# An attention-and-FFN kernel: k, q and v loaded first, x formed earlier in the order, float32 w_out for two more items

## The chip, the cores and the metric

The program runs on one core of a Trainium2 chip. Its engines are PE (TensorE, the matmuls, with a queue of its own for loading weights, PEld), DVE (VectorE), ACT (ScalarE), POOL (GpSimd) and SP (SyncE, which here only issues DMAs). Each takes its own instructions strictly in the order in which they were queued when the kernel was built, and waits where an instruction's data aren't there yet. The metric is the device time of one execution in microseconds.

## The reference

Attention with a softmax of q over the head's features and a softmax of k over the sequence, and on its result a feed-forward layer:

```
q_s = exp(q - max(q, axis=-1));  q_s = q_s / (sum(q_s, axis=-1) + 1e-09)
k_s = exp(k - max(k, axis=2));   k_s = k_s / (sum(k_s, axis=2) + 1e-09)
kv  = einsum('bhsd,bhse->bhde', k_s, v)
x   = einsum('bhsd,bhde->bhse', q_s, kv)        # then (B*S, H*D)
h   = x @ w_in
g   = h * erf(max(h, 0) + log1p(exp(-abs(h))))  # erf of softplus
out = g @ w_out
```

There are 8 batches, 8 heads, 576 rows and 64 features, so x is 4608 x 512; w_in is 512 x 2048 and w_out 2048 x 512. Inputs q, k and v are float32. The weights arrive as float64 and are read as pairs of int32.

## The kernel before

**Work items.** The 4608 rows of x are cut into 12 blocks of 384 tokens (three for each pair of batches), and the 2048 hidden columns into 4 groups g of 512. A block and a group make a work item n; there are 48, four in a row for each block. An item has these steps: `m n.0` to `m n.3` (mm1, the product with w_in, into tile H), T and G (softplus and erf on ACT, into tile G), U (gmul on DVE: G times H), I and O (ghi and glo on DVE, which split G into two float16 tiles that lie in H's place), and `M n.0` to `M n.2` (mm2, the product with w_out, for three tiles of 128 tokens, summed over the block's four items in the PSUM banks o0 to o2).

**Two arithmetics.** Items 0 to 3 (the first block) are computed wholly in float32, with the decoded weights as they are (mm1_32 L912, mm2 L988). All others use weights and x split into a high and a low float16 part. mm1 is then seven products of half-size blocks (L873, twelve 128x192 matmuls each, into banks pX, pY and pZ, evacuated at L885 to L900 by DVE and ACT in turn), and mm2 has 36 matmuls an item (L997).

**The weights.** Each of the eight weight groups (jobs 0 to 7: in 0, in 1, out 0, in 2, out 1, in 3, out 2, out 3) is loaded as two pieces of 1 MB (wload, L182) and decoded from float64 bits to float32 by three DVE operations a piece (L198, L202, L205; step `D job.piece`). ACT squares them for their maxima (Q, L230), and when all eight are squared, Z (wscales) computes the scales: a reduction (L240), transposes (L245), further reductions (L249) and a row of tiny operations (L252 to L273). Then each group is split (S: high part on ACT at L278, low part on DVE at L279) and, for w_in, the sums of blocks that the seven products need are formed (R, L304). Items 4 on can't start before Z, S0 and R0.

**Attention.** The opening (function start) treats batch 0: per half of the heads q is reduced and normalised (L758, L442 to L448), the maximum of k over the sequence is taken (k_max, L477 and L480), turned by PE and reduced (kT L487, km L491, kB L500), subtracted (L745, L747), exponentiated (L754), and k is multiplied with v (kv, L521), normalised (kvbd, L550) and multiplied with the transposed q (qT L596, x L605) into x (L424). Batches 1 to 7 go through a generator whose pieces are called off by `A` in the order list, and later by a pace.

**What sets the order.** The string ORDER lists the steps up to item 3, SPLITS the splits behind items 4 to 6, and a loop the rest. A scheduler moves instructions within each engine's queue from there. SP's DMAs share eight semaphores, so that each waits for the eighth before it. H has three buffers, G two, and the pool `at` gives two to each tag.

Of the kernel before, what the change touches and what calls it, by code (L numbers as in the profile page):

```python
# [53 lines left out]
def attn_moe_kernel(  # L54
# [54 lines left out]
    WT = [  # L109
        cp.tile([P, 2 * (7 if which == "in" else 4) * 512], F16, name=f"wt{i}")  # L110
        for i, (which, g) in enumerate(JOBS)
    ]
# [39 lines left out]
    slots += [None, 0, 1, *range(4, 2 * NG), -1]  # L152

    def wload():

# [2 lines left out]
        while i < NPC * NJ and slots:
            w = slots.pop(0)
            if i >= NPC * (NJ - 1 if w is None else NJ if w < 2 else w - 2):  # L160
                continue
            if w == -1:
                w, other = None, "x7"
            else:
                other = None
            which, g = wjobs[i // NPC]
            a = i % NPC
            if which == "in":
                src = w_in[a * 2 * P:(a + 1) * 2 * P, 2 * g * 512:2 * (g + 1) * 512]
            else:  # L170
                src = w_out[(4 * g + 2 * a) * P:(4 * g + 2 * a + 2) * P, :]
            if other:

                raws[i] = xp.tile([P, 2, 1024], I32, tag=other, name=f"raw_{i}")
            elif w is None:
                raws[i] = rp.tile([P, 2, 1024], I32, tag="raw", bufs=1, name=f"raw_{i}")
            else:
                raws[i] = WT[w][:, :4096].bitcast(I32).rearrange("p (a n) -> p a n", a=2)
            held[i] = -1 if other else w

            eng = nc.sync if i < LOADS.count("w") else nc.gpsimd
            eng.dma_start(raws[i], src.rearrange("(a p) n -> p a n", p=P))  # L182
            nxt[0] += 1
            return
# [964 lines left out]
```

## Time and profile before

| What | Value |
|---|---|
| Times of three runs | 886.32, 883.01, 882.18 us (median 883.01) |
| Profiled execution: its own time, and the span in the trace | 886.16 us, 884.3 us |
| Mean granted TensorE clock | 0.983 |
| PE, DVE, ACT, POOL busy | 828.4, 656.3, 504.6, 17.7 us |
| DMA traffic | 55.52 MB, mean 63 GB/s |
| First f32 matmul of item 0 | 34.40 us |
| First mm2 of item 0 | 58.75 us |
| First f16 matmul of item 4 | 137.80 us |

Times in the trace are counted from the span's start. A busy PE says that a matmul was under way, not that it ran at full rate: the granted clock stands beside it. [...]

### The profile page before, as it was taken

How to read it: one execution, taken by the hardware profiler on the slowest of the kernel's cores; microseconds unless marked ns; L12 is line 12 of the kernel's file. 1: busy time of each engine (PE TensorE's matmuls, PEld its weight loads, DVE VectorE, ACT ScalarE, POOL GpSimd, SP SyncE). 2: the span in 40 equal slices, each digit the busy share in tenths (PEclk: the TensorE clock that was granted, in tenths of full speed). 3: DMA queues.
4: the chain of work that ended last, by engine and by line, in shares of the span. 5: the costliest groups of instructions: out<-in, count | busy, mean ns of one | idle time of the engine just before them, and what ended most of it. 6: DMA issues, size and time to landing. Idle time of an engine off the chain costs nothing.

```text
span 884.3 us, 15529 instructions
## 1 busy us (share of the span) xinstructions
PE 828.4 (94%) x6556; PEld 571.0 (65%) x6556; DVE 656.3 (74%) x901; ACT 504.6 (57%) x645; POOL 17.7 (2%) x37
## 2 busy tenths in 40 slices
PE   2899995799989989999999999999999999999997
PEld 1555553666657757767767667767776677676763
DVE  7899669998978696876886596877885565744453
ACT  2487376786565645644754646645745546453632
POOL 2100100000000000000000000000000000000000
PEclk9899997799999999999999999999999999999999
DMA  9984720013105120421023111311010000000100
GB/s 274 408 186 137 178 47 37 1 40 81 43 24 114 37 60 10 94 61 25 14 72 79 36 49 25 90 48 25 13 49 1 13 24 2 27 11 1 36 1 36
DMA packets 117381, 55.52 MB, mean 63 GB/s; under 512 B 106561, under 2 KB 108609, under 8 KB 117313
## 3 DMA queue, kind: packets, MB, share of 16 engines
q1 hardware_dynamic: 115136, 46.15, 20.2%
q0 software_dynamic: 2176, 8.39, 2.6%
q8 instruction: 51, 0.84, 0.4%
q14 instruction: 18, 0.14, 0.1%
HBM read 45.09 MB, written 9.44 MB: 62 GB/s over the span
## 4 chain that ended last, share of the span: by engine, by line
PE 67%; DVE 19%; ACT 9%; issue 2%; DMA 2%; SPq 1%; ACTq 0%; DVEq 0%
PE o L997 27%; PE pX L873 15%; PE pZ L873 7%; PE o L988 4%; ACT G L326 4%; PE pY L873 3%; ACT L326 3%; DVE G L952 3%; DVE H L969 2%; PE kv L521 2%; DVE kmax L477 2%; PE pX L912 2%; DVE wt L279 2%; PE qT L596 1%; DVE H L965 1%
## 5 line engine op out<-in xcount | busy, mean ns | idle before, releaser
L997 PE MATMUL o<-wt,H 128*128 128x512 f16 x1584 | 367.7, 381 | 3.2 <-DVE H L965 2.3
L873 PEld LDWEIGHTS <-wt 128*128 128x128 f16 x3696 | 312.8, 99 | 50.3 <-issue 18.8
L997 PEld LDWEIGHTS <-H 128*128 128x128 f16 x1584 | 152.8, 98 | 159.6 <-DVE H L965 3.3
L873 PE MATMUL pX<-x,wt 128*128 128x192 f16 x2112 | 207.5, 249 | 9.4 <-DVE H L887 3.6
L326 ACT ACT_TABLE_LOAD x104 | 133.4, 1283 | 11.9 <-DVE H L898 7.2
L952 DVE SCALAR_TENSOR_TENSOR G<-G,small,H 128x1536 f32<-128x1536 f32 x44 | 79.9, 1816 | 67.0 <-ACT G L326 66.9
L873 PE MATMUL pZ<-x,wt 128*128 128x192 f16 x1056 | 105.6, 250 | 8.7 <-ACT H L890 4.5
L900 ACT COPY H<-pX 128x384 f32<-128x384 f32 x44 | 21.0, 476 | 131.4 <-PE pX L873 131.4
L326 ACT ACTIVATE G<-H,U 128x768 f32<-128x768 f32 (+1 forms) x60 | 73.0, 1232 | 25.7 <-DVE H L898 25.1
L969 DVE TENSOR_TENSOR H<-G,H 128x1536 f16<-128x1536 f32 x44 | 77.2, 1756 | 1.1
L326 ACT ACTIVATE G<-G 128x1536 f32<-128x1536 f32 x48 | 71.3, 1484 | 0.5
L873 PE MATMUL pY<-x,wt 128*128 128x192 f16 x528 | 51.6, 246 | 3.5 <-ACT wt L278 2.0
L424 ACT ACTIVATE x<-x 128x384 f32<-128x384 f32 (+1 forms) x52 | 17.6, 386 | 55.4 <-PE x L608 53.3
L885 DVE COPY H<-pY 128x384 f32<-128x384 f32 x44 | 24.3, 553 | 28.8 <-PE pY L873 28.8
L278 ACT ACTIVATE x<-x 128x768 f16<-128x768 f32 (+1 forms) x44 | 32.9, 762 | 21.5 <-DVE x L370 21.4
L965 DVE CAST H<-G 128x1536 f16<-128x1536 f32 x44 | 42.0, 955 | 0.8
L279 DVE SCALAR_TENSOR_TENSOR x<-x,x 128x768 f16<-128x768 f32 (+1 forms) x44 | 37.2, 848 | 3.5 <-ACT x L278 3.4
L1013 DVE TENSOR_SCALAR ob<-o,V 128x512 f32<-128x512 f32 x29 | 21.7, 747 | 23.7 <-PE o L997 23.6
L898 DVE TENSOR_TENSOR H<-pZ,H 128x384 f32<-128x384 f32 x44 | 24.2, 551 | 19.6 <-PE pZ L873 19.5
L887 DVE TENSOR_TENSOR H<-pX,H 128x384 f32<-128x384 f32 x44 | 24.4, 554 | 14.8 <-PE pX L873 14.4
L370 DVE TENSOR_TENSOR x<-x 128x384 f32<-128x384 f32 x44 | 24.2, 550 | 8.5 <-ACT x L424 8.1
L895 DVE TENSOR_TENSOR H<-pX,H 128x384 f32<-128x384 f32 x44 | 24.2, 550 | 4.5 <-PE pX L873 4.4
(160 smaller groups left out, 824.5 us busy)
## 6 DMA issues: line engine op xcount, KB each, us to landing
out_dram<-ob SPq DMA_DIRECT2D x32, 256.0 KB, 2.2
vbuf<-in_v_dram SPq DMA_DIRECT2D x60, 128.0 KB, 3.2
q<-in_q_dram SPq DMA_DIRECT2D x56, 128.0 KB, 3.0
k<-in_k_dram SPq DMA_DIRECT2D x56, 128.0 KB, 3.2
wt<-in_moe_w_out_dram POOLq DMA_DIRECT2D x5, 1024.0 KB, 6.7
wt<-in_moe_w_in_dram SPq DMA_DIRECT2D x4, 1024.0 KB, 8.7
raw<-in_moe_w_in_dram SPq DMA_DIRECT2D x2, 1024.0 KB, 16.4
wt<-in_moe_w_out_dram SPq DMA_DIRECT2D x2, 1024.0 KB, 13.5
```

Of the source, the lines that this page charges most:

```text
L278: nc.scalar.activation(hi, src, AF.Copy, scale=s)
L279: nc.vector.scalar_tensor_tensor(lo, src, s, hi, op0=ALU.mult, op1=ALU.subtract)
L326: i = nc.scalar.activation(out_, in_, func, **kw)
L370: nc.vector.tensor_tensor(Bk[o], Bk[a], Bk[b], op=ALU.subtract)
L873: nc.tensor.matmul(o, w[wl][:, c, a * P:(a + 1) * P], x[:, xl, xi, c, :], start=(new and a == 0 and c == 0 and i == 0), stop=(c == 1 and i ...
L885: nc.vector.tensor_copy(C[0, 0], bank2("Y"))
L887: add(C[0, 0], bank2("X"), C[0, 0], op=ALU.add)
L952: nc.vector.scalar_tensor_tensor(flat(s["G"]), flat(s["G"]), GA[:, g:g + 1], flat(s["H"]), op0=ALU.mult, op1=ALU.mult,)
L965: nc.vector.tensor_copy(flat(s["gh"]), flat(s["G"]))
L969: nc.vector.tensor_tensor(flat(s["gl"]), flat(s["G"]), flat(s["gh"]), op=ALU.subtract)
L988: nc.tensor.matmul(o, s["G"][:, a, ts_], w[:, a, :], start=(first_ and a == 0), stop=(last_ and a == FG - 1),)
L997: nc.tensor.matmul(o, s[gt][:, a, ts_], w[wl][:, a, :], start=(first_ and a == 0 and i == 0), stop=(last_ and a == FG - 1 and i == 2),)
```

## The change

Line numbers of the kernel after differ from those before; where a row of it is shown, its operation is named.

1. **Loads.** k, q and v are loaded ahead of all weights, and the first eight weight pieces behind them on SP. The ninth and tenth go through POOL's queue, the ninth at once behind the opening's memsets. Weight places are new tiles (four wi, five wo) and the free places are sorted by the time up to which they are free.
2. **k_max** takes two tensor-tensor maxima per half (128x512 and 128x256) instead of one strided reduction.
3. **The first weight piece of each half is decoded in two column halves**, and `m0.0` and `m0.1` need the first half only.
4. **x of batch 0** is formed from kvbd directly after the second normalisation. Its columns for block 0 are evacuated at once (x0 to x3), those for block 1 after the scale is known (y0 to y3). q of batch 0 is transposed into banks pX, pY, pZ and o2.
5. **Scales.** The squares go to a bfloat16 tile in SBUF, the transposes of Z to pY and pZ; a factor GB, for unsplit w_out, is added to the tiny operations. The scheduler places Z earlier (below).
6. **Items 4 and 5** (OUT32) multiply G with GB and w_out of groups 0 and 1 in float32, without ghi and glo. S2 and S4, the splits of these two groups, move behind items 7 and 8.

```diff
-LOADS = "qkwwvwwwwww"
+LOADS = "kqvwwwwwwww"
...
-    qm0 qm1 kmax kT kB qe0 qn0 ks2 ks0 D0.0 ks1 ke2 ke0 ke1 w6 kv0 kn0 D0.1 qe1 qn1 kv1 t0
-    kn1 kvs x0 t1 lkv t2 x2 t3 x1 x3
-    m0.0 D1.0 m0.1 D1.1 m0.2 m0.3 T0 G0 Q0
+    kmax qm0 kT kB qe0 qm1 ks2 ks0 ks1 ke2 ke0 ke1 qn0 t0 t1 qe1 qn1 w6 kv0 kn0 kv1 kn1
+    D0.0.0 D0.1.0 t2 t3 x0 x1 x2 x3 kvs lkv y0 y1 y2 y3
+    m0.0 m0.1 D0.0.1 D0.1.1 D1.0 D1.1 m0.2 m0.3 T0 G0 Q0
...
-    M2.0 M2.1 M2.2 M3.0 M3.1 M3.2 S1 R1 S2
+    M2.0 M2.1 M2.2 M3.0 M3.1 M3.2 S1 R1
...
-SPLITS = {4: "S3 R3 S4", 5: "S5 R5 S6", 6: "S7"}
+SPLITS = {4: "S3 R3", 5: "S5 R5 S6", 6: "S7", 7: "S2", 8: "S4"}
+
+OUT32 = range(4, 6)
+OUTS = [2, 3, 0, 1]
...
+        if part is None:
+            r = raws[i].rearrange("p a n -> p (a n)").rearrange("p (n two) -> p n two", two=2)
+        else:
+            r = raws[i][:, :, 512 * part:512 * part + 512].rearrange(
+                "p a (n two) -> p a n two", two=2
+            )
+            d = d.rearrange("p (a n) -> p a n", a=2)[:, :, 256 * part:256 * part + 256]
...
-                bank(f"sq_{jn}_{i}"), stg[jn][:, i * 512:(i + 1) * 512], AF.Square,
-                accum_out=sq4[:, o, i:i + 1],
+                sqs, stg[jn][:, i * 512:(i + 1) * 512], AF.Square, accum_out=sq4[:, o, i:i + 1]
...
-            bk = psa.tile([P, 512], F32, tag="bk", name=f"ws_{which}")
+            bk = psh.tile([P, 512], F32, tag="pY" if i == 0 else "pZ", name=f"ws_{which}")
...
+        nc.vector.tensor_scalar(
+            GB, w_u["in"], m[:, 0:1], m[:, 1:2], op0=ALU.mult, op1=ALU.mult
+        )
+        nc.vector.tensor_scalar_mul(GB, GB, 2.0**-20)
...
         kmax = at.tile([P, H, D], F32, tag="qT", name=f"kmax_{b}")
+        k2 = at.tile([P, 2, 4, D], F32, tag="qT", name=f"k2_{b}")
         for hf in range(2):
-            nc.vector.tensor_reduce(
-                kmax[:, hf * 4:hf * 4 + 4, :], ks[hf], axis=AX.X, op=ALU.max
+            nc.vector.tensor_tensor(k2, ks[hf][:, 0:2], ks[hf][:, 2:4], op=ALU.max)
+            nc.vector.tensor_tensor(
+                kmax[:, hf * 4:hf * 4 + 4, :], k2[:, 0], k2[:, 1], op=ALU.max
             )
...
         def xc(c):
-            bk = pso.tile([P, 512], F32, tag=f"o{(c + 1) % 2}", name=f"x_0_{c}")
+            name = f"x_0_{c}"
+            bk = pso.tile([P, 512], F32, tag=f"o{c}", name=name) if c < 3 else bank(name)
             x_mm(0, c, bk, r[f"t{c}"])
-            x_split(0, c, bk)
+            x_split(0, c, bk, slice(1))
+            put(f"x{c}", bk)
...
-            steps[f"x{i}"] = (f"t{i} kvs", lambda i=i: xc(i))
+            steps[f"x{i}"] = (f"t{i} kn1", lambda i=i: xc(i))
+
+            steps[f"y{i}"] = (f"x{i} kvs", lambda i=i: x_split(0, i, r[f"x{i}"], slice(1, 9)))
...
+        assert "all" in wready
         nc.vector.scalar_tensor_tensor(
-            flat(s["G"]), flat(s["G"]), GA[:, g:g + 1], flat(s["H"]),
+            flat(s["G"]), flat(s["G"]), (GB if n in OUT32 else GA)[:, g:g + 1], flat(s["H"]),
             op0=ALU.mult, op1=ALU.mult,
         )
-        assert "all" in wready
+        if n in OUT32:
+            return
...
-        if n < NG:
+        if n < NG or n in OUT32:
             w = stg[jn].rearrange("p (a e) -> p a e", a=FG)
...
-            if 4 < n <= N and i < 2:
+            if 4 < n <= N and i < 2 and n - 1 not in OUT32:
                 tok(f"{'IO'[i]}{n - 1}")
```

**First place: DVE's queue at the start of the program.** A row has the line, the operation, what it writes and reads (buffer 101 holds the first raw half of q before, and the first of k after; 103, 105 and 107 hold the other halves; km is the reduced turned maximum), and the shape. Before:

```order
L758 TENSOR_REDUCE q_0_0_m_141<-H_raw_0_0_101 128x16
L759 TENSOR_TENSOR q_0_0_137<-H_raw_0_0_101,q_0_0_m_141 128x1024
L758 TENSOR_REDUCE q_0_1_m_144<-G_raw_0_1_103 128x16
L477 TENSOR_REDUCE kmax_0_147<-H_raw_0_0_105 128x256
L477 TENSOR_REDUCE kmax_0_147<-H_raw_0_1_107 128x256
L442 TENSOR_REDUCE q_0_0_r_164<-q_0_0_137 128x16
L480 TENSOR_TENSOR kmax_0_147<-kmax_0_147,kt_0_109 64x512
```

and after:

```order
L496 TENSOR_TENSOR k2_0_140<-H_raw_0_0_101 128x512
L497 TENSOR_TENSOR kmax_0_139<-k2_0_140 128x256
L496 TENSOR_TENSOR k2_0_140<-H_raw_0_1_103 128x512
L497 TENSOR_TENSOR kmax_0_139<-k2_0_140 128x256
L500 TENSOR_TENSOR kmax_0_139<-kmax_0_139,kt_0_105 64x512
L511 TENSOR_REDUCE km_0_154<-kT_0_149 128x4
L782 TENSOR_REDUCE q_0_0_m_146<-H_raw_0_q_100 128x16
```

The chain of k now stands first, and q's reductions behind it; the two reductions of k have become two pairs of maxima.

**Second place: DVE's queue where the scales are computed**, beside items 2 and 3 (small holds the scales, sq4 the squares, ws are the turned maxima, wse their steps, x_1 and x7_1 the x of block 1, and q_2_0 and q_2_1 the halves of q of batch 2; the last number of a name is the buffer). Before:

```order
L435 TENSOR_REDUCE q_2_1_m_1225<-q_2_1_782 128x16
L436 TENSOR_TENSOR q_2_1_782<-q_2_1_782,q_2_1_m_1225 128x1024
L240 TENSOR_REDUCE small_84<-sq4_100 128x8
L279 SCALAR_TENSOR_TENSOR x7_1_861<-x_1_140,x7_1_861 128x384
L249 TENSOR_REDUCE wse_in_822<-ws_in_817 128x4
L249 TENSOR_REDUCE wse_out_834<-ws_out_829 128x4
L252 TENSOR_SCALAR wse_in_822<-wse_in_822 128x4
```

and after:

```order
L988 TENSOR_TENSOR G_3_698<-G_3_698,H_3_664 128x1536
L297 SCALAR_TENSOR_TENSOR x7_1_837<-x_1_138,x7_1_837 128x768
L252 TENSOR_REDUCE small_81<-sq4_98 128x8
L387 TENSOR_TENSOR x_1_138<-x_1_138 128x2x192
L262 TENSOR_REDUCE wse_in_796<-ws_in_791 128x4
L262 TENSOR_REDUCE wse_out_808<-ws_out_803 128x4
L265 TENSOR_SCALAR wse_in_796<-wse_in_796 128x4
L453 TENSOR_REDUCE q_2_0_m_1092<-q_2_0_741 128x16
L266 TENSOR_SCALAR wse_in_796<-wse_in_796 128x4
```

The reduction of the squares (L240, now L252) stood behind both halves of batch 2's q; now it stands ahead of them, just behind the product of item 3 (L988), and the reduction of the first half (L453) stands between the scales' small operations.

**Third place: ACT's queue at item 9** (its copies of pZ and pX into H_9, table load and softplus; x_3 is the x of block 3, and x7_3 its split for item 12). Before:

```order
L890 COPY H_9_1784<-pZ_9_1837 128x2x192
L278 ACTIVATE x7_3_1978<-x_3_1639 128x768
L892 COPY H_9_1784<-pX_9_1799 128x2x192
L278 ACTIVATE x7_3_1978<-x_3_1639 128x384
L278 ACTIVATE x7_3_1978<-x_3_1639 128x768 x2
L900 COPY H_9_1784<-pX_9_1799 128x2x192
```

and after:

```order
L928 COPY H_9_1711<-pZ_9_1764 128x2x192
L296 ACTIVATE x7_3_1908<-x_3_1564 128x768
L930 COPY H_9_1711<-pX_9_1726 128x2x192
L296 ACTIVATE x7_3_1908<-x_3_1564 128x384
L938 COPY H_9_1711<-pX_9_1726 128x2x192
L343 ACT_TABLE_LOAD
L343 ACTIVATE G_9_1874<-H_9_1711,U_1_645 128x1536
L296 ACTIVATE x7_3_1908<-x_3_1564 128x768
```

The item's last copy (L900, now L938) stood behind two further splits of x (L278); they have moved behind it.

More of the change, by code (lines that the diff above doesn't have):

```diff
@@ L105, in attn_moe_kernel @@
         kvbd.append(t)
[L109 to L112, printed above, removed]
+    WI = [cp.tile([P, 2 * 7 * 512], F16, name=f"wi{g}") for g in range(NG)]
+    WO = [cp.tile([P, 2 * 4 * 512], F16, name=f"wo{g}") for g in range(NG + 1)]
+    wplace = {("out", g): WO[([NG] + OUTS)[OUTS.index(g)]] for g in range(NG)}
+    wplace |= {("in", g): WI[g] for g in range(NG)}
+    raw_place = {("out", g): WO[g] for g in range(NG)}
+    raw_place |= {("in", g): WI[g + 1] for g in range(NG - 1)}
     WIN = 7 * 512
@@ L154, in wload @@
+    slots.sort(key=lambda x: x[1])
     def wload():
         i = nxt[0]
[L158 to L163, printed above, removed]
-            else:
[L165 to L184, printed above, removed]
@@ L186, in wdecode @@
-    def wdecode(i):
-        jn, a = divmod(i, NPC)
-        if a == 0:
-            if jn + 2 < NJ:
-                stg[jn] = WT[jn + 2][:, :4096].bitcast(F32)
-            elif jn == NJ - 2:
+        if i == NPC * NJ:
+            return
+        while slots and i >= slots[0][1]:
+            slots.pop(0)
+        if not slots:
+            return
+        place, end = slots.pop(0)
+        which, g = wjobs[i // NPC]
+        a = i % NPC
+        if which == "in":
+            src = w_in[a * 2 * P:(a + 1) * 2 * P, 2 * g * 512:2 * (g + 1) * 512]
+        else:
+            src = w_out[(4 * g + 2 * a) * P:(4 * g + 2 * a + 2) * P, :]
@@ new lines, in wload, with wdecode @@
+        if place == "x7":
+            place = xp.tile([P, 4096], F16, tag="x7", name=f"raw_{i}")
+        raws[i] = place[:, :4096].bitcast(I32).rearrange("p (a n) -> p a n", a=2)
+        held[i] = [place, end]
+        eng = nc.sync if i < LOADS.count("w") else nc.gpsimd
+        eng.dma_start(raws[i], src.rearrange("(a p) n -> p a n", p=P))
+        nxt[0] += 1
+    def wdecode(i, part=None):
+        jn, a = divmod(i, NPC)
+        if jn not in stg:
+            if wjobs[jn] in raw_place:
+                stg[jn] = raw_place[wjobs[jn]][:, :4096].bitcast(F32)
+            else:
@@ L287, in wsplit @@
         s = w_s[which][:, g:g + 1]
-        assert "all" in wready and not raws and jn == nsplit[0]
-        nsplit[0] += 1
+        assert "all" in wready and not raws
+        assert all(wplace[wjobs[jn]] is not raw_place.get(wjobs[j]) for j in stg)
         if which == "out":
@@ L610, in x_mm, with x_split @@
             )
-    def x_split(b, c, bk):
-        for blk, off, o, w in xcols(b, 0 if b % 2 == 0 else SM + 2 * TAIL, SM):
+    def x_split(b, c, bk, part=None):
+        for blk, off, o, w in xcols(b, 0 if b % 2 == 0 else SM + 2 * TAIL, SM)[part or slice(9)]:
             x_put(
@@ L623, in attention @@
         ks, qs, kt = d["k"], d["q"], even["kt"][tl]
-        kmax = k_max(b, [t.rearrange("p t h d -> p h d t") for t in ks], (kt, tl))
+        kmax = k_max(b, ks, (kt, tl))
         yield SHARES[0]
@@ L782, in start @@
         steps = {
-            "kmax": ("", lambda: put("kmax", k_max(
-                0, [t.rearrange("p h t d -> p h d t") for t in kx], (kt, tl)))),
+            "kmax": ("", lambda: put("kmax", k_max(0, perm, (kt, tl)))),
             "kT": ("kmax", lambda: put("km", k_max_T(0, r["kmax"]))),
```

68 lines of the change are left out of this document (43 added, 25 removed).

## The prediction

> **What bounds the kernel now.** First the page: busy shares, then the slices over time.
>
> ```profile
> PE 828.4 (94%) x6556; PEld 571.0 (65%) x6556; DVE 656.3 (74%) x901; ACT 504.6 (57%) x645; POOL 17.7 (2%) x37
> PE   2899995799989989999999999999999999999997
> PEclk9899997799999999999999999999999999999999
> ```
>
> PE bounds, but not evenly: its empty slices are the first, and those around 145 to 175 us, where the granted clock is low too. The windows view gives this by stage (busy us and instructions of each engine, then clock, DMA share and GB/s). The borders are mine: item 0's first matmuls, its mm2 (58.8), the end of item 3's mm2 (135.2), the ends of mm1 of items 4, 5 and 7, and a hole at 244.
>
> ```profile
> 0.00:28.80 28.80, 9.32 (x100) 7.12 (x100) 23.40 (x28) 6.14 (x6) 7.37 (x17) 0.99 1.03 306
> 28.80:34.20 5.40, 4.68 (x15) 3.16 (x16) 3.46 (x8) 1.49 (x3) 0.00 (x0) 0.50 1.03 410
> 34.20:58.80 24.60, 24.60 (x77) 13.83 (x76) 24.43 (x29) 19.67 (x39) 1.43 (x2) 0.98 0.98 297
> 58.80:95.80 37.00, 35.76 (x170) 18.39 (x169) 36.51 (x49) 25.51 (x39) 3.14 (x5) 1.00 0.56 136
> 135.20:161.90 26.70, 15.00 (x107) 12.57 (x106) 24.99 (x45) 18.08 (x18) 0.00 (x0) 0.68 0.03 11
> 161.90:175.90 14.00, 9.51 (x88) 8.24 (x86) 13.76 (x16) 12.03 (x14) 0.00 (x0) 0.88 0.01 2
> 175.90:209.30 33.40, 32.43 (x313) 22.86 (x312) 33.16 (x66) 25.67 (x28) 0.63 (x2) 1.00 0.30 68
> 209.30:243.70 34.40, 33.03 (x255) 22.32 (x253) 31.50 (x35) 19.02 (x28) 0.00 (x0) 1.00 0.16 39
> 243.70:253.90 10.20, 7.46 (x50) 4.60 (x49) 6.65 (x13) 7.12 (x7) 0.00 (x0) 0.83 0.18 51
> 253.90:880.00 626.10, 617.21 (x5266) 436.71 (x5264) 433.31 (x588) 344.91 (x410) 2.53 (x8) 1.00 0.14 37
> ```
>
> From 254 us on PE is busy in 617 of 626 us at full clock: there only less PE work would help, and the change makes no less. PE loses time in four places: the opening (9.3 of 28.8 us busy), the weight scales and splits (135.2 to 175.9), a little behind them, and the hole at 244. In two of them (58.8 to 95.8, 161.9 to 209.3) DVE is busy for over 98% of the time, so DVE decides what PE finds ready.
>
> **The change part by part.** Four terms: opening, items 0 to 3, transition, hole.
>
> *Opening.* The chain to the first full-rate work, from the timeline (start, duration, and in brackets idle time and releaser):
>
> ```profile
> 4.89 1.22 DVE L758 TENSOR_REDUCE q_m<-H_raw 128x16 f32<-128x1024 f32 x1 [4.89 <-DMA H_raw<-in_q_dram]
> 8.54 3.80 DVE L477 TENSOR_REDUCE kmax<-H_raw 128x256 f32<-128x1024 f32 x2
> 13.39 0.68 DVE L480 TENSOR_TENSOR kmax<-kmax,kt 64x512 f32<-64x512 f32 x1
> 20.46 1.14 PE L521 MATMUL kv<-vbuf,k 128*64 128x65 f32 x16 [2.99 <-ACT k L754]
> 28.85 1.08 PE L596 MATMUL qT<-ident,q 128*128 128x128 f32 x4 [3.40 <-DVE kvbd L550]
> 58.75 2.74 PE L988 MATMUL o<-wt,G 128*128 128x512 f32 x6
> ```
>
> The first load lands at 4.9 us; it will be k's first half. The second, behind it in the same queue, I estimate at 6.4 and the short tail at 8 to 9. Four maxima and the tail's: no row has a 128x256 one, so between 0.19 (the smallest DVE operation quoted below, L240) and 0.68 (512 elements, the row at 13.39) each; I take 0.4, near half of the latter. The maximum is done at about 9.7 instead of 14.1. From there the chain (turn, reduce, broadcast, subtract, exponentiate) took 6.4 us to kv, but now q's reductions and subtractions (1.2 us each) stand between: in order on DVE and ACT, the second half of k is exponentiated at 21.4. kv is done at about 27, no sooner than before. The gain is behind it: q is transposed inside kv instead of behind it, x needs kvbd only and not the maximum and scale, and its evacuation for block 1 leaves the path. So PE is busy from about 27 on, without the hole of 3.4 us and without the half clock (0.50 at 28.8 to 34.2). The rest is a sum: transposes still open (some 1 us), x (four products of 128x512 at 0.86, worked out below: 3.4) and item 0's sixteen products of 128x384 at 0.645 (1.29 from start to start for two in the rows below: 10.3) bring 27.3 to 42.0; item 1's 10.3 more give 52.4 for the first mm2.
>
> ```profile
> 43.08 1.45 PE L912 MATMUL pY<-x,wt 128*128 128x384 f32 x4
> 44.37 1.45 PE L912 MATMUL pZ<-x,wt 128*128 128x384 f32 x4
> ```
>
> That is **-6.3 us** (58.75 to 52.4). U0, which mm2 waits for, comes out at 52.1 on DVE, since two maxima and subtractions of batch 1, and some decode operations, now stand behind it. Bounds: -4 if DVE, 24.43 of 24.60 us busy before, is 2 us late; -8 if kv is 2 us sooner.
>
> The Trainium skill ("TensorE: Matmul & The Clock Gate", Part 1) has the clock halved after an idle window of about 3.4 us and given back after as much of sustained work. The trace agrees with 0.50 behind the 3.40 us of idle at 28.85. The same page's Part 4 says that transposes don't count as busy: the early qT would then not hold the clock up. By that rule x and the first matmuls would run at half clock for up to 3.4 us, which would be some 1.7 us less gain; my bound of -4 holds it.
>
> The ninth weight piece (1 MB) goes into the opening's loads. At 306 to 410 GB/s (first windows) it takes 2.6 to 3.4 us of the engines' time. DVE's first decode is wanted at about 25.8, and I have the first two pieces landing at 17 to 21: hidden. The Trainium skill ("Trainium Kernel Development and Optimization", Key Constraints) speaks against the change here: queues of SP, ACT and POOL run on the same 16 DMA engines and interleave. By it this piece could delay k or q by up to those 3.4 us.
>
> *Items 0 to 3.* DVE takes up what moved behind U0, against two k_max sooner:
>
> ```profile
> L477 DVE TENSOR_REDUCE kmax<-k 128x256 f32<-128x1024 f32 x14 | 27.5, 1971 | 0.0
> ```
>
> Each half falls from 1.97 to about 1.1 (0.68 and 0.4). My walk through the queues finds stalls of 0.5 us at kT of batch 1 and 1.9 at its second v half, mostly covered: **+0.5** (0 to +2). Item 3's mm2 ends at about 129.4 instead of 135.2.
>
> *Transition.* From there to the end of mm1 of item 7 PE now takes 74.1 us (135.2 to 209.3). What it waits for there (us, times, longest), and DVE's rows:
>
> ```profile
> PE pZ L873 <- ACT H L890: 4.5, 2, 3.9
> PE pX L873 <- DVE H L887: 3.1, 1, 3.1
> 121.59 1.22 DVE L435 TENSOR_REDUCE q_m<-q 128x16 f32<-128x1024 f32 x1 [1.54 <-DMA q<-in_q_dram]
> 132.10 0.19 DVE L240 TENSOR_REDUCE small<-sq 128x8 f32<-128x32 f32 x1 [0.65 <-ACT sq L230]
> 138.51 3.13 DVE L279 SCALAR_TENSOR_TENSOR wt<-wt,small,wt 128x1024 f16<-128x1024 f32 x3
> 147.17 1.78 PE L873 MATMUL pZ<-x,wt 128*128 128x192 f16 x10 [1.92 <-DVE wt L279]
> ```
>
> Of these, 17.2 are idle (74.1 less 15.00, 9.51 and 32.43 busy), and low clock costs at least 5.9 more (15.00 x 0.32 and 9.51 x 0.12, from the windows). After the change the squares' reduction comes at about 114, before q of batch 2. But that q's reduction stands between the scales' operations, and its load is issued only at about 114.3 and lands 5 us later, so DVE sits idle for 3.4. The scales are ready at about 121.6, where now their first use on DVE is at 138.5, and the last split that item 4 waits for is done at 134.6 instead of 147.1. That does not free PE by 12.5: the end of item 3 comes only 5.9 sooner, and behind the splits the same DVE carries R, S, gmul and evacuations. There DVE loses ghi and glo of two items and the splits S2 and S4, and takes in batch 2's q and k. PE pays for float32: a 128x512 float32 tile has 8 records of 0.43 against 12 float16 of 0.216, from
>
> ```profile
> 129.63 3.17 PE L988 MATMUL o<-sg,G 128*128 128x512 f32 x7
> 132.64 0.60 PE L245 MATMUL ws_in<-ident,small 128*128 128x128 f32 x4
> 231.20 2.75 PE L997 MATMUL o<-wt,H 128*128 128x512 f16 x12
> 233.79 0.81 PE L608 MATMUL x<-qTs,kvbd 128*128 128x512 f16 x3
> L965 DVE CAST H<-G 128x1536 f16<-128x1536 f32 x44 | 42.0, 955 | 0.8
> L969 DVE TENSOR_TENSOR H<-G,H 128x1536 f16<-128x1536 f32 x44 | 77.2, 1756 | 1.1
> ```
>
> (3.01 for seven; 2.59 for twelve): 3.44 against 2.59, +0.85 for six tiles, **+5.1 us** of PE. DVE is relieved of 2 x (0.96 + 1.76) = 5.4, and of 2.3 for S4. The walk has mm1 of items 4 to 7 done at 148.5, 164 to 168, 188 to 190.6 and 201 to 204 (item 4 now at 161.9, item 7 at 209.3): the lost time falls by about 5.3, the float32's 5.1 take that back. Net **-0.2**; bounds -8 (13 of the lost time go, 5.1 come) and +5 (none goes).
>
> *Hole at 244.*
>
> ```profile
> 247.45 1.95 DVE L279 SCALAR_TENSOR_TENSOR x<-x,x 128x768 f16<-128x768 f32 x2
> 248.83 1.15 PE L873 MATMUL pX<-x,wt 128*128 128x192 f16 x12 [2.13 <-ACT H L900]
> 249.81 4.22 PE L997 MATMUL o<-wt,H 128*128 128x512 f16 x11
> ```
>
> 2.74 us idle (10.20 less 7.46), and a clock of 0.83 that costs 1.8: 4.5. ACT's copy of pX stood behind two further splits of x; it now stands ahead of them, and DVE's sums ahead of their low parts. **-3** (0 to -4.5).
>
> Later k_max takes less of DVE, which does not bound there; k2 shares two buffers with qT. 0 (-3 to +3).
>
> **Sum**: -6.3 + 0.5 - 0.2 - 3 = -9.0 on the profiled execution's 886.16: 877.2. That execution lies 3.15 above the median of the runs, so I predict **874.0** for the median.
>
> **The rivals.** *DVE takes the opening back.* It was busy for 36.51 of 37.00 us in 58.8 to 95.8 and now starts that stage with more queued. If item 3 ends no sooner, the 6.3 go: 880.3. For it: that row. Against: DVE works 24.52 of the next 39.40 us,
>
> ```profile
> 95.80:135.20 39.40, 39.40 (x134) 21.18 (x133) 24.52 (x35) 24.98 (x56) 2.62 (x3) 1.00 0.43 111
> ```
>
> so that its backlog can be worked off before item 3's end. *The transition fills better*: 13 of its lost time go instead of 5, 8 more than forecast: 866. For it: the scales come over 14 us sooner. Against: DVE, 98% busy there, stays in the way. *S2 and S4 overload items 8 to 11* (the other side): they move into 209 to 254, where DVE was 31.50 of 34.40 us busy. If each of four items then waits as at 244 (4.5), that is +18 less the 4.5 there, with -6 from the first three terms: 890.5. It decides once DVE has more than the 2.9 us free there; S4 takes 2.3, S2 as much, k_max gives back 1.7. *Weights late*: a piece took up to 24.3 us to land in the opening; if the first decode waits 12 us, the opening gains nothing and costs 3: 886.
>
> ```profile
> DMA to landing us min/median/max: 7.6/9.9/24.3
> ```
>
> If the change did not do what it says (k no sooner, say) the time would stay within 883, as in the first rival.
>
> **How the numbers follow.** Forecast (870 to 879) 0.5, DVE takes it back 0.18, transition better 0.13, overload 0.1, weights late 0.09. From the forecast's bounds and the neighbours: **864 to 886**, which leaves the overload and the ends out. A measurement of this kernel can tell about 0.5% (4.4 us) from no change. Faster by over that: nearly all of the forecast, a third of the first rival, all of the second, 0.67; within it 0.2; slower: the overload and a part of late weights, 0.13.
>
> **What would show it.** Right: the first mm2 of item 0 at about 52.4 at a clock near 1 from 27 us; item 3's end near 129; scales ready near 121.6; float32 mm2 of items 4 and 5 with 8 records of 0.43 a tile; no wait for the copy at item 9. Wrong: a first decode waiting for its load; PE waiting for gmul or decodes between 52 and 96; PE waiting for DVE at items 8 to 11; waits between items 4 and 7 well off 22 us.

## The result, and the profile after

The kernel after takes 860.78 us (858.32 to 862.41, four runs) beside 883.83 for the kernel before: a ratio of 0.9736 (95% interval 0.9719 to 0.9752). Faster, as forecast, but by 23 us instead of 9, and below the range. The page after, in the three rows shown of before (busy shares; busy tenths of PE; granted clock):

```profile
PE 825.6 (96%) x6532; PEld 569.2 (66%) x6532; DVE 637.1 (74%) x921; ACT 504.2 (59%) x645; POOL 17.6 (2%) x37
PE   3999997999999999999999999999999999999997
PEclk8999999999999999999999999999999999999999
```

The dip of PE and clock at 145 to 175 us is gone. Where the time went is read best at points that both kernels have: the first mm2, the end of item 3's mm2, and the copy on ACT that closes mm1 of an item (L900 before, L938 after).

| Point | Before | After | Shift | Step from the point above | Forecast of the step |
|---|---|---|---|---|---|
| first mm2 | 58.75 | 51.55 | -7.2 | -7.2 | -6.3 |
| end of item 3's mm2 | 135.20 | 127.37 | -7.8 | -0.6 | +0.5 |
| copy of item 7 | 209.53 | 191.38 | -18.2 | **-10.3** | **-0.2** |
| copy of item 9 | 248.32 | 225.93 | -22.4 | -4.2 | -3 |
| copy of item 14 | 336.73 | 314.40 | -22.3 | +0.1 | 0 |
| copy of item 47 | 862.19 | 838.55 | -23.6 | -1.3 | 0 |

I call the time from the first mm2 to the end of item 3's mm2 the stretch, and the time from there to the copy of item 7 the transition. The windows between these points, before and then after, where the opening's is shown too (columns as in the prediction):

```profile
58.75:135.20 76.45, 75.21 (x302) 39.61 (x301) 61.08 (x83) 50.49 (x95) 5.76 (x8) 1.00 0.49 123
135.20:209.50 74.30, 57.15 (x505) 43.86 (x504) 72.11 (x123) 55.77 (x60) 0.63 (x2) 0.86 0.15 35
```
```profile
0.00:28.80 28.80, 14.02 (x121) 11.16 (x122) 19.57 (x33) 8.82 (x12) 7.21 (x17) 0.82 1.03 307
51.55:127.37 75.82, 75.63 (x302) 39.38 (x301) 68.54 (x115) 57.96 (x97) 6.50 (x9) 1.00 0.56 148
127.37:191.40 64.03, 57.52 (x490) 42.31 (x489) 62.44 (x98) 48.65 (x54) 0.63 (x2) 0.97 0.18 44
```

The third number of busy time, DVE's, is the one to see. In the transition DVE is busy for 72.1 of 74.3 us before and 62.4 of 64.0 after: it got 10.3 us shorter, and DVE's work in it 9.7. In the stretch ahead of it DVE's work grew from 61.1 to 68.5 us, and that stretch got no longer: DVE had stood idle for 15 us there. The timeline of DVE after shows what moved:

```profile
111.44 0.19 DVE L252 TENSOR_REDUCE small<-sq 128x8 f32<-128x32 f32 x1 [2.99 <-ACT sqs L243]
114.23 1.22 DVE L453 TENSOR_REDUCE q_m<-q 128x16 f32<-128x1024 f32 x1 [0.27 <-DMA q<-in_q_dram]
118.72 1.94 DVE L297 SCALAR_TENSOR_TENSOR wi<-wi,small,wi 128x1024 f16<-128x1024 f32 x2
126.93 1.28 DVE L297 SCALAR_TENSOR_TENSOR wi<-wi,small,wi 128x1024 f16<-128x1024 f32 x1
```

The first row is the reduction of the squares, the second q's of batch 2, the third the first split of a weight: it starts at 118.72, 9 us before item 3's mm2 ends, where before the first use of the scales on DVE was at 138.5. The last row ends the splits of item 4's weights, at 128.2. So item 4 follows that mm2 on PE without a wait (timeline of PE, below), where before it waited for splits (1.92 us at 147.17, shown in the prediction, among others). What PE still waits for within item 4 is DVE's evacuations (1.55, 0.67 and 0.52 us):

```profile
117.07 10.46 PE L1028 MATMUL o<-wo,G 128*128 128x512 f32 x24
127.37 1.15 PE L911 MATMUL pY<-x,wi 128*128 128x192 f16 x12
148.51 2.08 PE L911 MATMUL pX<-x,wi 128*128 128x192 f16 x12 [3.05 <-ACT H L930]
```

Half clock is left in one place, from 148.5 to about 151.9 us (granted clock 0.50), behind the one wait of 3 us that is left: the group of twelve in the last row takes 2.08 us instead of 1.15.

### The profile page after: what moved, and what is told of

The parts are those of the page before. It is cut to its first block, busy times and chain, and to the rows that moved or that the text cites. A ratio compares the mean times of both kernels' runs of the same rounds, so it can differ in the third digit from the quotient of the medians.

```text
span 860.3 us, 15503 instructions
## 1 busy us (share of the span) xinstructions
PE 825.6 (96%) x6532; PEld 569.2 (66%) x6532; DVE 637.1 (74%) x921; ACT 504.2 (59%) x645; POOL 17.6 (2%) x37
## 4 chain that ended last, share of the span: by engine, by line
PE 67%; DVE 17%; ACT 10%; issue 2%; DMA 2%; SPq 1%; POOL 0%; ACTq 0%; DVEq 0%; POOLq 0%
PE o L1037 31%; PE pX L911 16%; PE pZ L911 8%; ACT G L343 4%; PE pY L911 4%; ACT L343 3%; PE kv L541 2%; DVE G L991 2%; PE x L631 2%; PE qT L616 2%; DVE H L1009 1%; DVE x L297 1%; PE o L1028 1%; DVE wi L297 1%; DVE H L1005 1%
## 5 line engine op out<-in xcount | busy, mean ns | idle before, releaser
L1037 PE MATMUL o<-wo,H 128*128 128x512 f16 x1512 | 348.0, 379 | 1.7 <-DVE H L1005 1.3
L911 PEld LDWEIGHTS <-wi 128*128 128x128 f16 x3696 | 309.5, 98 | 39.0 <-issue 17.4
L1037 PEld LDWEIGHTS <-H 128*128 128x128 f16 x1512 | 145.7, 98 | 150.1 <-DVE H L1005 1.8
L911 PE MATMUL pX<-x,wi 128*128 128x192 f16 x2112 | 204.8, 247 | 6.4 <-ACT H L930 3.0
L911 PE MATMUL pZ<-x,wi 128*128 128x192 f16 x1056 | 102.9, 246 | 0.9 <-DVE H L936 0.5
L938 ACT COPY H<-pX 128x384 f32<-128x384 f32 x44 | 20.9, 476 | 138.0 <-PE pX L911 133.0
L1009 DVE TENSOR_TENSOR H<-G,H 128x1536 f16<-128x1536 f32 x42 | 73.8, 1757 | 1.1
L1028 PE MATMUL o<-wo,G 128*128 128x512 f32 x144 | 66.7, 604 | 0.0
L911 PE MATMUL pY<-x,wi 128*128 128x192 f16 x528 | 51.8, 248 | 1.6 <-DVE H L923 1.6
L1028 PEld LDWEIGHTS o<-wo,G 128*128 128x128 f32 x144 | 26.3, 193 | 26.5 <-issue 25.8
L925 DVE TENSOR_TENSOR H<-pX,H 128x384 f32<-128x384 f32 x44 | 24.4, 555 | 15.3 <-PE pX L911 14.9
```

The lines of the kernel that those rows point to most:

```text
L911: nc.tensor.matmul(o, w[wl][:, c, a * P:(a + 1) * P], x[:, xl, xi, c, :], start=(new and a == 0 and c == 0 and i == 0), stop=(c == 1 and i ...
L925: add(C[0, 0], bank2("X"), C[0, 0], op=ALU.add)
L1009: nc.vector.tensor_tensor(flat(s["gl"]), flat(s["G"]), flat(s["gh"]), op=ALU.subtract)
L1028: nc.tensor.matmul(o, s["G"][:, a, ts_], w[:, a, :], start=(first_ and a == 0), stop=(last_ and a == FG - 1),)
L1037: nc.tensor.matmul(o, s[gt][:, a, ts_], w[wl][:, a, :], start=(first_ and a == 0 and i == 0), stop=(last_ and a == FG - 1 and i == 2),)
```

## The experiments

Kernels named a_ are the kernel after with one thing undone or added, those named b_ the kernel before with a part of the change. Times are medians of four runs; ratios are to the kernel before on the same chip (its medians lay between 884.07 and 884.60). The kernel after was run twice: its stretch is 75.8 us in both traces, its transition 64.0 and 65.0.

**The scales: squares in SBUF and the transposes in pY and pZ, alone and undone.** a_scales_back is this edit, b_scales its reverse in the kernel before:

```diff
-                sqs, stg[jn][:, i * 512:(i + 1) * 512], AF.Square, accum_out=sq4[:, o, i:i + 1]
+                bank(f"sq_{jn}_{i}"), stg[jn][:, i * 512:(i + 1) * 512], AF.Square,
+                accum_out=sq4[:, o, i:i + 1],
...
-            bk = psh.tile([P, 512], F32, tag="pY" if i == 0 else "pZ", name=f"ws_{which}")
+            bk = psa.tile([P, 512], F32, tag="bk", name=f"ws_{which}")
```

> The kernel before with one thing of the change alone: the squares go to a tile in SBUF and the transposes of the scales to banks pY and pZ, so that neither waits for the bank that the transposes of q use. Theory A (scales): the transition gained far more than forecast because this lets the reduction of the squares come before the product of item 3, so that item 4's splits run beside item 3's mm2. After gains 10.4 us between the end of item 3 and the end of mm1 of item 7, with 5.1 us of float32 matmuls added, so 15.5 us of lost time went; A expects -10 to -16 us here, 868 to 874, and PE's waits between item 3's end and item 7's mm1 cut by half. Theory B (float32 items): the relief of DVE by items 4 and 5 did it; B expects -3 to -5 here, 879 to 881.

> The kernel after with that one thing undone (squares and the scales' transposes in the bank that the transposes of q use). Theory A (scales): +10 to +16 us, 871 to 877, with PE waiting for the splits of item 4 again. Theory B (float32 items): +3 to +5, 864 to 866.

a_scales_back: 870.47, ratio 0.9836 (0.9816 to 0.9857): +9.7. b_scales: 880.06, 0.9949 (0.9932 to 0.9965): -4.5. The first is 0.3 short of theory A's range, the second fits B, so neither stands as stated. The windows of both show why (transition of a_scales_back; then the stretch of b_scales):

```profile
127.00:201.20 74.20, 62.91 (x481) 45.93 (x480) 70.41 (x124) 56.04 (x61) 0.63 (x2) 0.86 0.16 38
```
```profile
58.91:139.61 80.70, 76.91 (x302) 40.27 (x301) 70.79 (x121) 59.14 (x96) 5.75 (x8) 0.98 0.44 116
```

With the scales late again DVE's work in the transition is back at 70.4 us and the transition at 74.2, with float32 items and all. With the scales early alone the transition shrinks to 66.2, but the stretch ahead grows from 76.5 to 80.7. PE waits 2.5 us there for the reduction of the squares on DVE, which itself had waited 1.60 us for the last squares on ACT, and PE's granted clock is 0.98 instead of 1.00.

**Float32 items undone.**

```diff
-OUT32 = range(4, 6)
-OUTS = [2, 3, 0, 1]
+OUT32 = range(0)
+OUTS = [0, 1, 2, 3]
...
-    M2.0 M2.1 M2.2 M3.0 M3.1 M3.2 S1 R1
+    M2.0 M2.1 M2.2 M3.0 M3.1 M3.2 S1 R1 S2
...
-SPLITS = {4: "S3 R3", 5: "S5 R5 S6", 6: "S7", 7: "S2", 8: "S4"}
+SPLITS = {4: "S3 R3 S4", 5: "S5 R5 S6", 6: "S7"}
```

> The kernel after with items 4 and 5 in float16 again (ghi and glo are back, S2 behind item 3 and S4 behind item 4). Theory A (scales): PE gets 5.1 us back and DVE 5.4 us more to do; waits take back between nothing and all of it: 856 to 861. Theory B (float32 items): the waits of the kernel before return in part, +5 to +10: 866 to 871.

863.72, 0.9763 (0.9746 to 0.9779): +2.9, between the two theories.

```profile
126.40:196.00 69.60, 55.79 (x514) 41.72 (x513) 67.97 (x101) 49.26 (x54) 0.63 (x2) 0.93 0.17 41
```

DVE has 5.5 us more in the transition, and the transition is 4.6 to 5.6 longer than in the kernel after's two traces, though PE has less to do there. Some 2 to 4 us of that come back by item 14. One split, 2.35 us on DVE at 196.74, is left for that time in the kernel after; the float32 mm2 of items 4 and 5 is over there at 186.7. The rest of what comes back was not traced.

**The opening undone**: loads, the list up to the first mm2, and the functions xc and tc_ as before.

```diff
-LOADS = "kqvwwwwwwww"
+LOADS = "qkwwvwwwwww"
...
-    kmax qm0 kT kB qe0 qm1 ks2 ks0 ks1 ke2 ke0 ke1 qn0 t0 t1 qe1 qn1 w6 kv0 kn0 kv1 kn1
-    D0.0.0 D0.1.0 t2 t3 x0 x1 x2 x3 kvs lkv y0 y1 y2 y3
+    qm0 qm1 kmax kT kB qe0 qn0 ks2 ks0 D0.0 ks1 ke2 ke0 ke1 w6 kv0 kn0 D0.1 qe1 qn1 kv1 t0
+    kn1 kvs x0 t1 lkv t2 x2 t3 x1 x3
```

> The kernel after with the opening of before: loads, order of the steps up to the first mm1, x evacuated at once behind the split of kv, the first piece decoded whole. k_max, scales and float32 items stay. Theory A and B both: the opening's 7.2 us at the first mm2 are lost, 867 to 869. Rival C: DVE, not PE, sets when items 1 to 3 end, and takes a gain of the opening back: 860 to 863. Rival D: the sooner opening is also what lets the scales come in time: 872 or more.

869.19, 0.9824 (0.9796 to 0.9851): +8.4, 0.2 above what A and B expected, but not for their reason alone. The first mm2 is at 58.94 again, 7.4 later. The stretch is 80.6 us long, 4.8 longer (PE waits 3.7 us in it for the maximum of k of batch 1), and the transition, at 62.2, gives 2 to 3 back.

**The parts together, and the maximum of k.** b_opening is the kernel after with the edits of a_scales_back, a_no_out32 and a_kmax_back; b_opening_scales leaves out the first of these. a_kmax_back:

```diff
-            nc.vector.tensor_tensor(k2, ks[hf][:, 0:2], ks[hf][:, 2:4], op=ALU.max)
-            nc.vector.tensor_tensor(
-                kmax[:, hf * 4:hf * 4 + 4, :], k2[:, 0], k2[:, 1], op=ALU.max
+            nc.vector.tensor_reduce(
+                kmax[:, hf * 4:hf * 4 + 4, :], ks[hf].rearrange("p t h d -> p h d t"), axis=AX.X, op=ALU.max
             )
```

> The kernel after, unchanged, beside the other three on one chip, so that a few us can be compared. Both theories: 860 to 862.

> Of the change only the opening (loads, order up to the first mm2, halves of the first decode, x ahead of the split of kv) and the weight places; scales, k_max and items 4 and 5 as before. The scales alone gave -4.5 us, but undoing them in the kernel after cost +9.7; with the scales alone, and with the opening undone, the stretch of the float32 mm2 took 80.7 us where the kernel after takes 75.8. Theory E (the parts need each other): the scales' work falls on DVE during items 0 to 3, and PE waits there unless the opening has come sooner; what the opening gives by itself is then less than the 8.4 that undoing it cost: -3 to -6, 878 to 881. Rival F (parts add): -8 to -9, 875 to 876.

> Opening and scales together, without k_max and float32 items. Theory E (they need each other): -17 to -20 us, 864 to 867, and the stretch of items 0 to 3's mm2 at 76 to 77 us. Rival F (parts add: -4.5 and -8.4): -12 to -14, 870 to 872.

> The kernel after with the strided reduction for the maximum of k. If DVE is bound to it only in the opening and at the head of batches: the two halves of batch 0 cost 2 x 0.8 more in the opening, the later batches 1.3 in all (what the stretch from item 14 to the end gained): +2 to +4, 863 to 865. Rival G: it is hidden everywhere: within 1 of the kernel after, 860 to 862. Rival H: it takes DVE's slack beside the scales too: +5 or more, 866 up.

after_2: 860.88. b_opening: 881.10, 0.9959 (0.9944 to 0.9974), -3.4, as theory E had it. b_opening_scales: 877.61, 0.9931 (0.991 to 0.9953), -6.9: neither E nor F, less than the two parts gave singly (3.4 and 4.5), with a stretch of 82.4 us. a_kmax_back: 873.46, 0.9868 (0.9845 to 0.9891), **+12.6**, rival H, and far more than the 1.7 us of DVE that it costs a batch (DVE is busy for 650.7 us instead of 637.1, for eight batches). Its timeline, on PE and then DVE:

```profile
68.83 0.66 PE L505 MATMUL kT<-ident,kmax 128*128 128x128 f32 x4 [1.40 <-DVE kmax L498]
83.59 0.62 PE L539 MATMUL kv<-vbuf,k 128*64 128x65 f32 x13 [3.17 <-DMA vbuf<-in_v_dram]
```
```profile
87.30 0.16 DVE L558 TENSOR_SCALAR rd<-kv 128x2 f32<-128x2 f32 x1 [3.88 <-PE kv L539]
```

The issues of v's loads on SP's queue, in a_kmax_back and then in the kernel after:

```profile
76.45 2.56 SPq L408 DMA_DIRECT2D vbuf<-in_v_dram  x4
```
```profile
74.16 3.00 SPq L408 DMA_DIRECT2D vbuf<-in_v_dram  x4
```

k of batch 1 is a little later, so PE's first kv of batch 1 and, when it has freed the buffer, this load of v come 2.3 us later. That alone would make PE wait for nothing: the load has as long as in the kernel after, some 3.7 us, until PE wants it. But it lands only 7.1 us after its issue, and a weight piece of 1 MB lands beside it. DVE's last decode step of the piece before, which frees that one's buffer, shows why, in a_kmax_back and then in the kernel after:

```profile
75.38 1.23 DVE L215 SCALAR_TENSOR_TENSOR wo<-raw,wo 128x1024 int32<-128x1024 int32 x1
```
```profile
67.76 1.23 DVE L215 SCALAR_TENSOR_TENSOR wo<-raw,wo 128x1024 int32<-128x1024 int32 x1
```

In the kernel after this step stands ahead of the reduction of k's turned maximum in DVE's queue, in a_kmax_back behind k's subtraction. So POOL issues the next piece into that buffer at 76.91 instead of 69.28 us, half a microsecond behind v's load, and from 78 to 84 us the DMA engines are full (share 1.0 to 1.3). In the kernel after the piece is in at about 74.6, when v's load starts. PE waits for v, DVE stands idle behind PE, and the stretch takes 81.8 us instead of 75.8. The same two issues, half a microsecond apart, and the wait are in b_opening_scales (76.54 and 77.00, 3.8 us); where the scales are late, v's load is issued at 83.6 or later (a_scales_back, b_opening), away from the piece. That the piece is what delays v is read from these times; no run moved its load alone. Which batch matters was tried next, with k_max alone in the kernel before beside it:

```diff
+        if b == 1:
+            for hf in range(2):
+                nc.vector.tensor_reduce(
+                    kmax[:, hf * 4:hf * 4 + 4, :], ks[hf].rearrange("p t h d -> p h d t"), axis=AX.X, op=ALU.max
+                )
+            nc.vector.tensor_tensor(kmax[kt[1]], kmax[kt[1]], kt[0], op=ALU.max)
+            return kmax
```

> The kernel after with the strided maximum for batch 1 alone (two reductions of 1.95 us where the pairs take 2.2 in all). In the kernel with all eight strided, PE waited 1.4 us for this maximum and 3.2 for a load of v of batch 1, DVE stood idle 3.9 behind that, and the stretch of items 0 to 3's mm2 was 6.0 us longer. Theory K (knife edge in that stretch): batch 1 alone gives back half or more of the 12.6: 866 to 871. Rival L (every batch costs its part, 1.5 us each): 861 to 863.

> The kernel before with the new maximum of k alone. Undoing it in the kernel after cost 12.6 us. Theory E (the parts need each other): by itself it is worth little, since the kernel before waits for scales and splits behind it anyway: 0.9 in the opening, about 2 behind item 14, -2 to -5: 879.5 to 882.5. Rival H (DVE's time is worth that much wherever it is full): -9 or more, 875 or less.

a_kmax_b1: 867.44, 0.9810 (0.9795 to 0.9824), +6.6: half of the 12.6 comes from batch 1, theory K, with the two issues at 74.77 and 75.22 and the wait for v at 3.9 us. Its stretch is 83.6 us, so all that the stretch loses is batch 1's. The other half of the 12.6 lies elsewhere: against after_2, a_kmax_back's first mm2 is 2.0 us later, the transition 1.3 longer, items 8 and 9 1.7 longer, and 3.0 are lost behind them. b_kmax: 876.69, 0.9914 (0.9897 to 0.9930), -7.4: more than E and less than H expected. Its transition is as long as before (73.2), its first mm2 as late; it gains 1.5 in the stretch, 3.3 in items 8 and 9, the rest behind.

**A smaller delay of the scales, and a third float32 item.** a_ws_back undoes the second half of the scales' edit (the line with bank bk). a_three32:

```diff
-OUT32 = range(4, 6)
-OUTS = [2, 3, 0, 1]
+OUT32 = range(4, 7)
+OUTS = [3, 0, 1, 2]
...
-SPLITS = {4: "S3 R3", 5: "S5 R5 S6", 6: "S7", 7: "S2", 8: "S4"}
+SPLITS = {4: "S3 R3", 5: "S5 R5", 6: "S7", 7: "S2", 8: "S4", 9: "S6"}
```

> The kernel after with the squares in SBUF but the scales' transposes in the bank that the transposes of q use. DVE's queue then has both the reduction and the subtraction of q of batch 2 ahead of the scales, which would come 2 to 4 us later. Theory M (the time of the scales passes on to item 4 one for one, as it does in the kernel with both undone, where they come 13 us later and the time is 9.7 longer): +1.5 to +4, 862.5 to 865. Rival N (the squares alone matter, a few us of the scales are slack): 860 to 862.

> The kernel after with items 4, 5 and 6 in float32 (the split of w_out's group 2 behind item 9). PE gets 2.6 us more, DVE 2.7 and the 2.3 of a split less between items 4 and 7. If DVE still holds PE there (PE waits 9.6 us from 125 to 253 us): 857 to 861. If the two float32 items already use up what DVE's relief can give: 862 to 864.

a_ws_back: 863.78, 0.9766 (0.9749 to 0.9783), +3.0. The first split comes 4.5 us later; item 4 is not delayed (139.56 against 139.75), so M's one for one is wrong, but DVE's work in the transition is 65.3 us and the transition 66.4. a_three32: 864.71, 0.9777 (0.976 to 0.9794), +3.8: 0.7 beyond the range of the second theory, that two float32 items already use up the relief. Its transition is 65.6, and items 8 and 9 take 36.0 us instead of 34.4 to 34.6.

**Work added to DVE, and taken from it.** a_g5, a_g2 and a_g20 add to gmul of item 5, 2 or 20:

```diff
+        if n == 5:
+            for _ in range(2):
+                nc.vector.tensor_tensor(flat(s["G"]), flat(s["G"]), flat(s["G"]), op=ALU.max)
```

and a_pool_sums changes, in the splits,

```diff
-            nc.vector.tensor_tensor(A[o], A[x], A[y], op=op)
+            (nc.gpsimd if jn in (3, 5) else nc.vector).tensor_tensor(A[o], A[x], A[y], op=op)
```

> The kernel after with two more DVE operations on item 5's G (each a maximum of G with itself, 128x1536, 1.76 us in the kernel after's rows; G is not changed), just ahead of gmul. Theory P (DVE's work sets the transition's length): +3.4 at the end of mm1 of item 7 and +2.5 to +3.5 in the time, 863.5 to 864.5. Theory Q (single waits set it, the work fits into gaps): 0 to +1, 860.5 to 862.

> Control: the same two operations on item 2's G, in the stretch of items 0 to 3's mm2, where DVE is busy for 68.5 of 75.8 us and has its idle time at the end (102 to 112 us). Theory P, since the time to spare comes behind: 0 to +1.5, 861 to 862.5. If this stretch has its knife edge here too, as with the maximum of batch 1: +4 or more.

> Control: the same two operations on item 20's G, where DVE is busy for about 70% and PE does not wait. Both theories: 860.5 to 861.5.

> The kernel after with the four sums of the splits of w_in's groups 2 and 3 (eight operations of 128x512, 0.68 us each on DVE, 4.9 from start to start) on POOL, which stands idle there; nothing else is changed. Theory P: -3 to -5 in the transition, 856 to 858. Theory Q: the splits' high parts on ACT wait for the sums (4.4 us, three times, in the kernel after), and sums on POOL take longer: 861 to 864.

a_g5: 862.17, 0.9756 (0.9737 to 0.9775), +1.3 over after_2. Up to item 5's copy its trace keeps after_2's times within 0.1 us; then item 7's copy is 2.7 later for 3.4 us of work (P), but 1.5 of that is regained by item 14, so the total is 0.2 above Q's range and 1.3 below P's. a_g2: 862.56, 0.9761 (0.9746 to 0.9776), +1.7. The stretch is no longer (75.4 us), but the work pushes others behind: DVE's work in the transition is 67.9 us, and the transition 70.0; item 7's copy is 4.7 later than in after_2, and 2.6 of that is regained by item 14. a_g20: 862.78, 0.9765 (0.9744 to 0.9786), +1.9, where nothing was expected; in its trace 3.3 us of delay against after_2 stand at the first mm2 already, long before item 20 (see the last section), so it says how far two kernels with one opening can lie apart. Differences of up to some 2 us between two of these medians therefore show nothing by themselves; here the times within the traces carry the argument. a_pool_sums: 869.96, 0.9843 (0.9829 to 0.9858), **+9.1**, against P and beyond Q's range. Its timeline of POOL and DVE, then its waits (total, times, longest), then the groups by line and shape of the kernel after, with the mean in ns behind the bar, and a sum in its timeline:

```profile
142.04 8.09 POOL L321 TENSOR_TENSOR wi<-wi 128x512 f32<-128x512 f32 x4 [23.88 <-DVE wi L297]
142.35 2.05 DVE L454 TENSOR_TENSOR q<-q,q_m 128x1024 f32<-128x1024 f32 x1
144.31 3.35 DVE L297 SCALAR_TENSOR_TENSOR wo<-wo,small,wo 128x2048 f16<-128x2048 f32 x1
```
```profile
PE pZ L911 <- ACT H L928: 10.7, 1, 10.7
```
```profile
L454 DVE TENSOR_TENSOR q<-q,q_m 128x1024 f32<-128x1024 f32 x14 | 17.1, 1222 | 0.1
L297 DVE SCALAR_TENSOR_TENSOR wo<-wo,small,wo 128x2048 f16<-128x2048 f32 x4 | 9.4, 2347 | 0.0
```
```profile
131.92 0.68 DVE L321 TENSOR_TENSOR wi<-wi 128x512 f32<-128x512 f32 x1
```

Four sums take 8.09 us on POOL, where one takes 0.68 on DVE: the first and the last 1.27 and 1.26 each, the two beside DVE's operations 2.14 and 3.19. Those two operations on DVE take 2.05 and 3.35 instead of 1.22 and 2.35. ACT, which takes its splits in order, waits 5.2 us for these four sums, and PE waits 10.7 us for a copy that stands behind those splits on ACT. So DVE's work is what the transition is made of only while the chains through ACT aren't made longer. This run is no clean test of taking work away from DVE; that less work makes the transition shorter is seen in the parts of the change alone.

**Two tries at a better version**, a_split_late and then a_one32:

```diff
-SPLITS = {4: "S3 R3", 5: "S5 R5 S6", 6: "S7", 7: "S2", 8: "S4"}
+SPLITS = {4: "S3 R3", 5: "S5 R5 S6", 6: "S7", 9: "S2", 10: "S4"}
```
```diff
-SPLITS = {4: "S3 R3", 5: "S5 R5 S6", 6: "S7", 7: "S2", 8: "S4"}
+SPLITS = {4: "S3 R3 S4", 5: "S5 R5 S6", 6: "S7", 7: "S2"}
...
-OUT32 = range(4, 6)
-OUTS = [2, 3, 0, 1]
+OUT32 = range(4, 5)
+OUTS = [1, 2, 3, 0]
```

> The kernel after with S2 behind item 9 and S4 behind item 10. If the two splits (2.35 us each on DVE) overload items 8 and 9, where DVE is busy for 18.1 of 18.5 us: -1 to -3, 858 to 860. If not: 860.5 to 861.5.

> The kernel after with item 4 alone in float32 (S4 behind item 4 again, S2 behind item 7). PE gets 2.55 us back, DVE 2.7 and a split of 2.35 more within the transition. Two float32 items gave 2.9 over none in the time, three lost 3.8 over two. If the second item is worth what the first is: 862 to 863. If the first gives it all: 859 to 861.

a_split_late: 862.11, 0.9748 (0.9733 to 0.9762). a_one32: 862.77, 0.9762 (0.974 to 0.9783). Neither beats the kernel after, and both lie within the 2 us that a_g20 shows. Items 8 and 9 take 34.3 us in the first and 34.6 in the kernel after, but this does not test whether the splits overload them: the scheduler put the four w_out splits at nearly the same places as in the kernel after (the third at 187.83 and the fourth at 198.80, in after_2 at 182.82 and 196.65, where this trace runs 2 us later).

## Why the prediction was wrong, point by point

- **Opening, right.** The first mm2 stands at 51.55 (forecast 52.4), kT at 8.68, and x at full clock, 0.43 us a record, from 26.8. (A float32 matmul stands as two records in these traces: the four of x are eight records, four here and four at 30.04 us. A float32 transpose is one record.)

```profile
8.68 1.08 PE L507 MATMUL kT<-ident,kmax 128*128 128x128 f32 x4 [8.68 <-DVE kmax L500]
26.82 1.88 PE L628 MATMUL x<-qTs,kvbd 128*128 128x512 f32 x4
```

  The first weights were there in time. In this trace x runs at 0.43 us a record right behind the transposes of q, so what I had allowed for behind the rule on transposes (the Trainium skill, "TensorE: Matmul & The Clock Gate", Part 4: transposes don't count as busy for the clock) did not come. That doesn't refute the rule: kv's matmuls ran just ahead of them, and no trace here shows transposes alone.
- **Items 0 to 3, right in sum (-0.6 against +0.5), wrong in weight.** The two stalls that my walk found there (0.5 us at kT, 1.9 at v) did not come: PE is busy for 75.63 of 75.82 us. So that the sum is close is in part luck. I priced k_max at its DVE time. It is worth 12.6 us in the finished kernel, half of it in batch 1, through one load of v in this stretch. What the rival "DVE takes the opening back" forecast, item 3 ending no sooner, came true in the three kernels with opening and early scales that lack the new k_max in whole or for batch 1: item 3's mm2 ends at 134.3 to 135.0 there, against 135.2 before.
- **Transition, the step that failed.** "The lost time falls by about 5.3, the float32's 5.1 take that back. Net -0.2": it was -10.3, outside my bounds too. I had walked item 4's path from single waits: scales at 121.6, split done at 134.6, mm1 at 148.5, which is 19.1 us behind the end of item 3's mm2. The first split started at 118.72 and the last was done at 128.2, from 127.4 on item 4 waited for none, and the last copy of its mm1 stands at 139.75, 12.4 behind that end. So 6.7 us of the miss are in item 4 alone. By the prediction's own terms 17.8 us of lost time were to be left in the transition (17.2 and 5.9, less 5.3; the 22 among its signs don't follow from these); 8.2 were (6.5 idle, and 57.52 x 0.03 of low clock). One step of the walk is seen to be wrong, from SP's queue in the timeline:

```profile
109.14 8.11 SPq L408 DMA_DIRECT2D q<-in_q_dram  x8
```

  q's load was issued at 109 and not at 114.3, so that DVE did not stand idle for it (0.27 us instead of 3.4). The larger fault is the method. The rows that I quoted had DVE busy for 71.9 of 74.1 us there and idle for 14.9 of 39.4 just ahead, and the change moved the scales by 20 us into that idle time. Counting DVE's work instead gives nearly the whole: 72.1 us before and 62.4 after, 9.7 of the 10.3. With the scales undone it is 8.0 more and with the float32 items undone 5.5, together more than the 9.7, so these don't simply add. The count is made in the traces of after, not from the plan, so it says which sum would have served and not that it would have been found. The kernels bear it out: with late scales the transition was 73 to 81 us, with early scales and float16 items 66 to 71, with early scales and two or three float32 items 62 to 66 (68.7 with one, 67.7 and 70.0 in a_g5 and a_g2 with work added to DVE, 74.7 with the sums on POOL). Apart from a_pool_sums DVE was idle in it for 1.1 to 4.3 us.
- **Float32 items, right in price (8 records of 0.43 us a tile, as forecast), too low in relief**: undoing them makes the transition about 5 us longer. With late scales it is 74.2 us long in spite of them; what it would be there without them no run shows.
- **Hole, right, and for the reason given.** Of the -4.2, 2.9 are between the copies of items 8 and 9, where -3 was forecast. ACT's queue decides it. In the three kernels where splits of x still stand ahead of item 9's last copy, b_opening, b_opening_scales and a_kmax_back (first rows; the kernel after's copy, with no further split ahead of it, is in the second), PE still waits 1.3 to 1.7 us for that copy and the step takes 17.5 to 17.9 us (18.9 before); in all others 15.3 to 16.6.

```profile
234.79 0.84 ACT L296 ACTIVATE x<-x 128x768 f16<-128x768 f32 x1 [6.87 <-DVE x L387]
235.91 0.84 ACT L296 ACTIVATE x<-x 128x768 f16<-128x768 f32 x1 [0.28 <-DVE x L387]
236.66 0.46 ACT L936 COPY H<-pX 128x384 f32<-128x384 f32 x1
```
```profile
225.93 0.48 ACT L938 COPY H<-pX 128x384 f32<-128x384 f32 x1 [7.38 <-PE pX L911]
```

- **Rivals.** "The transition fills better" was the right kind and most of the size: 8 us more than forecast, where 10.1 were measured. The overload of items 8 to 11 did not come.

The parts don't add: undone singly they cost 8.4, 9.7, 12.6 and 2.9 us (33.6), of a whole of 23; opening, scales and k_max alone gain 3.4, 4.5 and 7.4. With early scales the stretch keeps its 75.8 us only where opening and new k_max are both there; where one or both are missing it takes 80.6 to 83.6, for a different wait in each case (v's load, k's maximum, the squares). Whether the float32 items need early scales is not shown: they were not run in the kernel before, nor were they taken out of a kernel with opening, k_max and late scales. The two halves of the scales' edit were only partly taken apart.
